# v's block means reach batch 0's last four token tiles by two DMAs, and the later weights are issued behind these

## The chip, the cores and the metric

The kernel runs on one core of a Trainium2 chip. A core has four compute engines that run their own instruction queues: TensorE (PE in the profile, with its weight loads as PEld), VectorE (DVE), ScalarE (ACT) and GpSimd (POOL). SyncE (SP) issues nearly all DMAs, in order: an issue whose condition isn't met holds up every issue behind it. The metric is the device time of one execution in microseconds, the median of several runs.

## The reference

Three blocks follow each other, for 2 batches of 768 tokens. First an attention with 8 heads of 64: each token sees the keys less than 16 away from it, and beside these 24 block summaries, one for each block of 32 keys (the maximum of the keys, the mean of the values). Then a feed-forward block with a token shift (512 to 1024 to 512) and a gate; then a mixer over tokens (768 to 256 to 768) and one over channels (512 to 1536 to 512).

```python
k_sum = k.reshape(B, H, nb, block, D).max(axis=3)
v_sum = v.reshape(B, H, nb, block, D).mean(axis=3)
scores_all = np.concatenate([scores_l_m, scores_s], axis=-1)   # local, then summaries
a = softmax(scores_all); out = a @ np.concatenate([v, v_sum], axis=2)
xk = mu_k * x + (1.0 - mu_k) * x_prev
k = np.maximum(xk @ w_k, 0.0); v = k * k @ w_v
r = sigmoid(xr @ w_r); x = r * v
u = x + (np.maximum(x.T @ w_tok1, 0.0) @ w_tok2).T
out = u + np.maximum(u @ w_ch1, 0.0) @ w_ch2
```

## The kernel before

**Tiles and stages.** A batch is 6 token tiles of 128. In the attention a unit of batch 0 is one token tile with every other head (`e` = 0 or 1), 12 units in all; a unit of batch 1 is a token tile with both. A unit passes through these steps: scores on TensorE (`sp`, L367), a masked read with row maxima on VectorE (L385), exponentials on ScalarE (L387), four transposes on TensorE (`pt`, L405) and their copy out of PSUM (`PT`, L408 on ScalarE for `e` = 0, L410 on VectorE for `e` = 1), and the products with the values (`pv`, L425). In batch 0 the sums of the softmax are divided out at the end (`rb`, L441, and the normalised tile `xT`, L445); in batch 1 GpSimd scales the probabilities (L399). Scores have two PSUM banks.

**Values and their means.** Each half of a token tile needs its own matrix of 120 rows: 96 rows of v (64 tokens and 16 more on either side) and 24 rows of block means. For batch 0 the 12 matrices lie in `ybuf`, two for a token tile. `vw_load` (L329) brings v's 96 rows. The means come from one sum of v over blocks (`vt_sum`, `v_gather`), which gives `vs`, 24 x 512, and `copy_sums` puts `vs` into each matrix, at row 0 or 96: token tile 0 by ScalarE, the others by GpSimd (first half, L345) and VectorE (second half, L343). In batch 1 each matrix gets its means by a DMA of its own.

**Weights.** They come as 64-bit floats. A piece of 128 x 512 is 512 KB; `Weights.load` (L137) issues its DMA on SP, and `Weights.step` turns it into a pair of 32-bit pieces, high and low: a prelude on ScalarE (L153), two integer operations on VectorE (L157, L163), the high half on ScalarE (L174) and the low half on GpSimd (L175). A product is three matmuls (high by high, high by low, low by high). The first 16 pieces are w_k (even numbers) and w_v (odd numbers) of the feed-forward block. `mixed` prepares that block's input (tmp on GpSimd L530, xk and xl on VectorE, xh on ScalarE); its products are ko (with w_k) and acc (with w_v); between them stand rl (VectorE), kh (ScalarE) and kl (GpSimd, L556).

**What sets the order.** The program is written stage by stage, with generators that interleave attention and feed-forward block; the framework then sorts the instructions of each engine by its own estimate of times and by the priorities that `ahead` gives. Engines run in the resulting order. The DMAs of SP use eight semaphores in turn, so each waits for the end of the one eight before it. In the order before, SP issues keys, queries and v for the first token tiles, then for each of the token tiles 2 to 5 two weights, two v halves and a q tile, then the other eight weights, then batch 1's keys, queries and values.

Of the kernel before, what the change touches and what calls it, by code (L numbers as in the profile page):

```python
# [30 lines left out]
AHEAD = 4  # L31
SPIN0 = 7
SPIN, SPIN_UNITS = 1, 8
WFIRST = 2
S2COST, S3COST, S4COST = 4, 2, 3
PT_ACT = ((0, 0), (1, 0), (1, 1))
GB = 4
# [12 lines left out]
AHEAD3 = 2  # L50
WF = 2
HC = 256
VSUM = 0, 2
OB = 2

# [2 lines left out]
def fused_kernel(ctx, tc, q, k, v, vt, mu, w_k, w_v, w_r, w_t1, w_t2, w_c1, w_c2, out):  # L58
    nc = tc.nc
    B, NT = q.shape[:2]  # L60
    S, DM = v.shape[1] - WINDOW * 2, v.shape[2]
# [5 lines left out]
    NB = S // BLOCK  # L67
# [13 lines left out]
    def bank(tag, bufs, shape, name):  # L81
        return ps.tile(shape, F32, tag=tag, bufs=bufs, name=name)
# [10 lines left out]
    ybuf = ypool.tile([128, B * NT, DM], F32, name="ybuf")  # L93
# [6 lines left out]
    class Slot:  # L100


        def __init__(self, pl, tag):
            self.pl, self.tag = pl, tag
# [16 lines left out]
    class Weights:  # L121


        def __init__(self):
            self.todo, self.loaded, self.rounded, self.pin, self.ahead = [], [], [], 0, AHEAD
            self.early = True

        def add(self, slot, src, use):
            self.todo.append((slot, src, use))
# [1 line left out]
        def load(self):  # L131
            if self.todo:
                slot, src, use = self.todo.pop(0)
                slot = slot.next()
                st = slot.tile([128, 512], I64, "wst")
                w = src.shape[2] if len(src.shape) > 2 else 0
                d = nc.sync.dma_start(st.rearrange("p (a n) -> p a n", n=w) if w else st, src)  # L137
                if PINW:
                    after(d)
                self.loaded.append((slot, st, use))  # L140

        def step(self):
# [35 lines left out]
    def pieces(slot, name):  # L178
        return [x.rearrange("p (a n) -> p a n", n=HC) for x in slot.split(name)]

    def sums(pair, eng, *ops, adder=nc.vector):
        s = stage.tile([128, 512], F32, tag="wf", bufs=WF, name="sum")
        s = s.rearrange("p (a n) -> p a n", n=HC)
        for a, x, y, op in ops:
# [42 lines left out]
    def behind(inst, marks):  # L227

        for m in marks:
            tc.add_manual_dep(inst.ins, m.ins.name,  # L230
                              mybir.DependencyInfo(mybir.DependencyClass.NoSync, mybir.DependencyReason.DATA), reason="queue order")

    def after(inst):

        behind(inst, mark[-1:])

    weights = Weights()
# [17 lines left out]
    def ahead(n):  # L255

        def wrap(fn):
            def run(*args, **kw):
                with tc.high_priority(n) if n else ExitStack():
                    return fn(*args, **kw)  # L260
            return run
        return wrap

    state = {}
# [24 lines left out]
    @ahead(HK)  # L289
    def kw_sums(b, t):  # L290
        st = state[b]
        for o in (0, WC - NB):
            nc.gpsimd.tensor_scalar(st["kw"][t][:, :, o:o + NB], st["ks"], 1.0, 1.0, ALU.mult, ALU.mult)
# [10 lines left out]
    @ahead(HR)  # L304
    def vt_sum(b, j):
        st = state[b]
        if j == 0:
            st["vr"] = at.tile([128, NP, NB], F32, tag="vrs", bufs=1, name="vrs")
        r = nc.vector.tensor_reduce(st["vr"][:, 2 * j:2 * j + 2], st.pop(("vt", j)), AX.X, ALU.add)
        if b == 0:  # L310
            behind(r, lows[-1:])

    @ahead(HR)
    def v_gather(b):
        st = state[b]
        vp = bank("pt", 2, [128, NP, 128], "vp")
        for p in range(NP):
            nc.tensor.transpose(vp[:NB, p], st["vr"][:, p], ident)
        st["vs"] = at.tile([NB, DM], F32, tag="vs", bufs=1, name="vs")
        nc.scalar.activation(st["vs"], vp[:NB].rearrange("p g e -> p (g e)"), AF.Copy, scale=1.0 / BLOCK)  # L320

    @ahead(HL)
    def vw_load(b, t):
        ws = []
        for half in range(2):
            w = ybuf[:NC, 2 * t + half] if b == 0 else at.tile([NC, DM], F32, tag="vw", bufs=VB, name="vw")
            row, srow = (NB, 0) if half == 0 else (0, NK)
            key = 128 * t + 64 * half
            after(nc.sync.dma_start(w[row:row + NK], v[b, key:key + NK]))  # L329
            ws.append((w, srow))  # L330
        st_of(b)["vw"][t] = ws

    def vw_sums(b, t):
        ahead(HV if b or t == 0 else 0)(copy_sums)(b, t)

    def copy_sums(b, t):
        for j, (w, srow) in enumerate(state[b]["vw"][t]):
            if b:
                nc.sync.dma_start(w[srow:srow + NB], state[b]["vs"])
            elif t == 0:  # L340
                nc.scalar.copy(w[srow:srow + NB], state[b]["vs"])
            elif j:
                nc.vector.tensor_copy(w[srow:srow + NB], state[b]["vs"])  # L343
            else:
                nc.gpsimd.tensor_copy(w[srow:srow + NB], state[b]["vs"])  # L345

    @ahead(HL)
    def q_load(b, t):
# [100 lines left out]
    def attention():  # L449
        slots = {}  # L450
        n0 = 2 * NT
        steps = [(0, t, (e,)) for t in range(NT) for e in range(2)] + [(b, t, (0, 1)) for b in range(1, B) for t in range(NT)]
        for i in range(len(steps) + 1):
            if i < len(steps):
                b, t, es = steps[i]
                if b and t == 0:
                    yield from prep(b)
                zs = s_stage(b, t, es)
                if len(es) == 1:
                    for what, z, lag in zip((t_stage, v_stage), (zs[0], zs), LAGS):  # L460
                        slots.setdefault(min(i + lag, n0), []).append(((i + lag, lag), what, z))
                else:
                    slots[i + 1] = [((i, 1), n_stage, z) for z in zs] + [((i, 2), t_stage, z) for z in zs] + [((i, 3), v_stage, zs)]
                if i < SPIN_UNITS:
                    spin(SPIN)
                yield 0.95 * len(es)
                if es[-1] == 1 and t + 1 < NT:
                    kw_sums(b, t + 1)
                if b and t == 0:
                    vw_sums(b, 0)  # L470
                if i in VSUM:
                    vt_sum(0, VSUM.index(i))
                if i == VSUM[1]:
                    v_gather(0)
                    vw_sums(0, 0)
            for _, what, z in sorted(slots.get(i, ()), key=lambda s: s[0]):
                what(z)
                if what is t_stage:
                    yield 0.43
                elif what is v_stage:  # L480
                    yield 0.7 * len(z)
                    done_tiles[0] += len(z) / 2
            if i < len(steps):
                if 0 in es:
                    if t + 1 < NT and t + 1 not in state[b]["vw"]:
                        vw_load(b, t + 1)
                    if b and t + 2 < NT:
                        q_load(b, t + 2)
                if i == VSUM[1]:
                    vw_sums(0, 1)  # L490
                elif 1 in es and t + 1 < NT and i > VSUM[1]:
                    vw_sums(b, t + 1)
                if b + 1 < B:
                    for e in es:
                        prep_next(b + 1, 2 * t + e)
# [16 lines left out]
    def prep(b):  # L512

        for t in range(NT):
            k_max(b, t)
            yield HOLD / (NT + 2)
        for j in range(2):
            vt_sum(b, j)
            yield HOLD / (NT + 2)
        kw_sums(b, 0)  # L520
        v_gather(b)
# [23 lines left out]
    def cut(p, a, n):  # L545
        return p[0][:, a:a + n], p[1][:, a:a + n]
# [69 lines left out]
    def spin(n):  # L616

        o = bank("ko", 1, [128, 4, 128], "spin")
        for _ in range(n):
            after(nc.tensor.matmul(o, ident, ident.unsqueeze(1).to_broadcast([128, 4, 128]), start=True, stop=True))  # L620
# [13 lines left out]
    for t in range(2, NT):  # L634
        for _ in range(WFIRST):
            weights.load()
        vw_load(0, t)
        if t + 1 < NT:
            q_load(0, t + 1)
    while weights.todo:  # L640
        weights.load()
    masks = []
    for kind in range(3):
        mc = at.tile([128, NC], F32, name=f"mask{kind}")
# [96 lines left out]
    def c1_src(g, z):  # L741
        return w_c1[z * 128:(z + 1) * 128, :].rearrange("p (h f) -> p h f", h=2)[:, :, HC * g:HC * g + HC]

# [88 lines left out]
    def new_f4():  # L832
        return w2.tile([128, 4, HC], F32, tag="f4", bufs=2, name="f4")

# [85 lines left out]
    def d_phase(uu):  # L920
# [9 lines left out]
        def part(i, g, uu):  # L930
            seq[0] += 1
            o = bank(*(("ko", 1), ("pv", 1), ("pt", 2), ("pt", 2))[seq[0] % 4], [128, 2, HC], "m")
            while (i, 1) not in c1[g]:
# [5 lines left out]
        def values2(pr, c, g, fh, th, last=False):  # L939
# [6 lines left out]
            for j, f in enumerate(fs):  # L946
                wh, wl = c2[c, f]
                for n in range(2):
                    t = 2 * th + n
                    gh, gl = cut(pr, j * HC + n * 128, 128)  # L950
                    for i, (l, r) in enumerate(((gh, wh), (gh, wl), (gl, wh))):
# [188 lines left out]
```

## Time and profile before

| | |
|---|---|
| median of 3 runs | 505.56 us (503.67 to 506.71) |
| the profiled execution | 506.84 us |
| its span, first to last instruction | 504.9 us |
| TensorE busy | 489.1 us, 97% |
| VectorE / ScalarE / GpSimd busy | 319.6 / 239.7 / 240.0 us |
| mean granted clock of TensorE | 0.989 |

A share of busy time is a mean over stages. TensorE is full almost everywhere, so what can move the end is its idle time and the time at a lower clock; both lie in the first 100 us, but for the last few. A waiting engine names what released it last, and a DMA issue is shown on SP with the time at which it left.

### The profile page before, as it was taken

Reading aid. Unit: us, or ns where it says so; the run is one execution under the profiler, and the core shown is the slowest. Engines: PE = TensorE matmul, PEld = TensorE weight load, DVE = VectorE, ACT = ScalarE, POOL = GpSimd, SP = SyncE. Lnnn points to the kernel's source line nnn. Section 1 sums busy time; section 2 is a strip of 40 time slices with the busy share of each in tenths; the row PEclk is TensorE's granted clock in tenths of the full one; section 3 lists DMA queues with packets and bytes.
Section 4 is the critical chain, followed back from the end, with each engine's and each line's share of the span. In section 5 each row is a group of like instructions: output and inputs, shape, how many; then the busy total and the mean of one; then the engine's idle time right before and its main releaser. Section 6 shows DMA issues by size and latency. Waiting matters only on the chain.

```text
span 504.9 us, 8793 instructions
## 1 busy us (share of the span) xinstructions
PE 489.1 (97%) x3278; PEld 407.0 (81%) x3278; DVE 319.6 (63%) x638; ACT 239.7 (47%) x541; POOL 240.0 (48%) x294
## 2 busy tenths in 40 slices
PE   7999997999999999999999999999999999999996
PEld 3567785888888898887887787878888999989995
DVE  3888998641514365698789789646479638354352
ACT  1778746872443545655456555554554435011110
POOL 5335587862543457488845535764941813000000
PEclk9899998899999999999999999999999999999999
DMA  8999940321000650000550999629351404163102
GB/s 265 298 294 345 345 124 13 89 80 40 20 1 1 233 186 0 1 0 7 162 167 5 386 398 329 215 91 320 132 167 42 140 30 167 51 201 112 56 1 83
DMA packets 35914, 70.63 MB, mean 140 GB/s; under 512 B 3072, under 2 KB 12288, under 8 KB 35872
## 3 DMA queue, kind: packets, MB, share of 16 engines
q1 hardware_dynamic: 34288, 69.09, 42.1%
q10 hardware_dynamic: 1584, 0.98, 0.7%
q8 instruction: 26, 0.43, 0.4%
q14 instruction: 16, 0.13, 0.1%
HBM read 60.04 MB, written 9.44 MB: 138 GB/s over the span
## 4 chain that ended last, share of the span: by engine, by line
PE 65%; DVE 14%; DMA 11%; ACT 4%; POOL 3%; issue 3%; SPq 1%; DVEq 0%; ACTq 0%; POOLq 0%
PE o L952 12%; PE ko L541 11%; PE m L541 11%; PE acc L541 10%; PE o L980 7%; PE go L541 5%; DMA wst<-in_moe_w_v_dram 4%; PE ro L541 3%; DVE wf L163 3%; DMA wst<-in_moe_w_ch_dram 2%; DMA xT<-in_vt_dram 2%; DVE xk L531 2%; PE pv L425 2%; PE sp L367 2%; DVE xl L533 2%
## 5 line engine op out<-in xcount | busy, mean ns | idle before, releaser
L175 POOL TENSOR_TENSOR w<-wf,w 128x512 fp32r<-128x512 f32 x50 | 69.0, 1387 | 60.8 <-ACT w L174 57.7
L541 PE MATMUL ko<-xh,w 128*128 128x256 f32 x384 | 76.4, 288 | 1.7 <-POOL w L175 0.9
L541 PE MATMUL m<-u,w 128*128 128x256 f32 x504 | 65.1, 283 | 0.7 <-DVE mw L843 0.7
L541 PEld LDWEIGHTS m<-u,w 128*128 128x128 f32 x504 | 63.4, 191 | 2.8 <-DVE mw L843 0.9
L541 PEld LDWEIGHTS ko<-xh,w 128*128 128x128 f32 x384 | 61.2, 188 | 5.4 <-POOL w L175 1.1
L541 PE MATMUL acc<-w,kh 128*128 128x512 f32 x192 | 61.4, 404 | 0.0
L952 PE MATMUL o<-w,gh 128*128 128x512 f32 x192 | 59.1, 391 | 0.0
L541 PE MATMUL ko<-xl,w 128*128 128x256 f32 x192 | 54.4, 283 | 1.1 <-DVE xl L533 1.1
L174 ACT CAST w<-wf 128x512 fp32r<-128x512 f32 x50 | 30.9, 620 | 50.3 <-DVE wf L163 48.5
L163 DVE SCALAR_TENSOR_TENSOR wf<-wst,wf 128x512 int32<-128x512 int32 x50 | 47.5, 958 | 8.8 <-ACT wst L153 7.7
L556 POOL TENSOR_TENSOR kl<-rl,kh 128x512 fp32r<-128x512 f32 x24 | 34.3, 1430 | 36.0 <-ACT kh L555 32.6
L530 POOL TENSOR_SCALAR tmp<-xT,oms 128x256 f32<-128x256 f32 x52 | 38.5, 748 | 21.2 <-DVE xk L531 12.4
L554 DVE TENSOR_TENSOR rl<-rl 128x512 f32<-128x512 f32 x24 | 18.7, 781 | 46.0 <-ACT rl L553 45.8
L387 ACT ACTIVATE pe<-pe,mn 128x120 f32<-128x120 f32 x96 | 36.6, 383 | 14.8 <-DVE mn L385 14.6
L531 DVE SCALAR_TENSOR_TENSOR xk<-xT,mus,tmp 128x256 f32<-128x256 f32 x52 | 39.3, 788 | 5.1 <-POOL tmp L530 4.7
L153 ACT ACTIVATE wst<-wst 128x512 f32<-128x512 f32 x62 | 40.9, 674 | 2.7 <-DMA wst<-in_moe_w_ch_dram 2.7
L541 PEld LDWEIGHTS acc<-w,kh 128*128 128x128 f32 x192 | 35.3, 192 | 7.3 <-ACT pe L387 0.3
L952 PEld LDWEIGHTS o<-w,gh 128*128 128x128 f32 x192 | 34.7, 188 | 6.2
L541 PE MATMUL acc<-w,kl 128*128 128x512 f32 x96 | 37.8, 404 | 0.9 <-POOL kl L556 0.9
L541 PEld LDWEIGHTS ko<-xl,w 128*128 128x128 f32 x192 | 36.2, 188 | 2.2 <-DVE xl L533 1.3
L952 PE MATMUL o<-w,gl 128*128 128x512 f32 x96 | 37.1, 391 | 0.0
L541 PE MATMUL go<-u,w 128*128 128x512 f32 x144 | 35.7, 393 | 0.0
(119 smaller groups left out, 950.9 us busy)
## 6 DMA issues: line engine op xcount, KB each, us to landing
wst<-in_moe_w_ch_dram SPq DMA_DIRECT2D x36, 512.0 KB, 7.3
w<-stored SPq DMA_DIRECT2D x24, 512.0 KB, 5.5
stored<-w SPq DMA_DIRECT2D x24, 256.0 KB, 4.8
wst<-in_moe_w_k_dram SPq DMA_DIRECT2D x8, 512.0 KB, 7.9
wst<-in_moe_w_v_dram SPq DMA_DIRECT2D x8, 512.0 KB, 9.9
wst<-in_moe_w_tok_dram SPq DMA_DIRECT2D x6, 512.0 KB, 4.9
out_dram<-o SPq DMA_DIRECT2D x12, 256.0 KB, 2.3
kw<-in_k_dram SPq DMA_DIRECT2D x9, 320.0 KB, 5.0
```

What stands on the lines that cost most here:

```text
L153: a = nc.scalar.activation(top.bitcast(F32), top.bitcast(F32), AF.Prelu, scale=2.0 ** -112, alpha=2.0 ** 32)
L163: nc.vector.scalar_tensor_tensor(wi, top, 3, wi, ALU.logical_shift_left, ALU.bitwise_or)
L174: r = nc.scalar.copy(hi, src)
L175: eng.tensor_tensor(lo, src, hi.bitcast(F32), ALU.subtract)
L387: nc.scalar.activation(pe, pe, AF.Exp, bias=mn[:, p:p + 1], scale=-1.0, accum_out=den[:, p:p + 1])
L530: nc.gpsimd.tensor_scalar(tmp, xT[:, d, x0 - 1:x0 - 1 + MW], om[:, d:d + 1], 1.0, ALU.mult, ALU.mult)
L531: nc.vector.scalar_tensor_tensor(xk[:, d], xT[:, d, x0:x0 + MW], mu[:, d:d + 1], tmp, ALU.mult, ALU.add)
L541: nc.tensor.matmul(o, l, r, start=(first and i == 0), stop=(last and i == 3 * n - 1))
L554: nc.vector.tensor_tensor(rl, rl, rl, ALU.mult)
L556: nc.gpsimd.tensor_tensor(lo, rl, hi.bitcast(F32), ALU.subtract)
L952: nc.tensor.matmul(accs[c][t], l, r, start=(first and j == 0 and i == 0), stop=(last and j == 1 and i == 2))
L980: nc.tensor.matmul(accs[0][t], l, r, start=(k == 0 and i == 0), stop=(k == NF2 - 1 and i == 2))
```

## The change

`copy_sums` still writes the means of token tile 0 by ScalarE and of tile 1 by GpSimd and VectorE. For token tiles 2 to 5 it issues, together with tile 0's copies, two DMAs on SP: one writes `vs` four times to row 0 of the four first halves, one to row 96 of the four second halves (192 KB each). The second for-loop of the start issues one weight instead of two ahead of each token tile's values; the remaining 12 are issued in the attention's third step, and each is put behind the second of the two DMAs in the queue (`gate`).

```diff
-WFIRST = 2
+WFIRST = 1
+TV = 2
...
                 if PINW:
                     after(d)
+                behind(d, self.gate)
...
     def copy_sums(b, t):
         for j, (w, srow) in enumerate(state[b]["vw"][t]):
+            vs = state[b]["vs"]
             if b:
-                nc.sync.dma_start(w[srow:srow + NB], state[b]["vs"])
+                nc.sync.dma_start(w[srow:srow + NB], vs)
             elif t == 0:
-                nc.scalar.copy(w[srow:srow + NB], state[b]["vs"])
+                nc.scalar.copy(w[srow:srow + NB], vs)
+                weights.gate = [nc.sync.dma_start(ybuf[srow:srow + NB, 2 * TV + j:2 * NT:2],
+                                                  vs.unsqueeze(1).to_broadcast([NB, NT - TV, DM]))]
...
                 if i == VSUM[1]:
                     v_gather(0)
                     vw_sums(0, 0)
+                    while weights.todo:
+                        weights.load()
...
                 if i == VSUM[1]:
-                    vw_sums(0, 1)
-                elif 1 in es and t + 1 < NT and i > VSUM[1]:
+                    for j in range(1, TV):
+                        vw_sums(0, j)
+                elif b and t + 1 < NT:
                     vw_sums(b, t + 1)
...
-    while weights.todo:
-        weights.load()
```

The order on SP is then: keys, queries, v of the first tiles; a weight, two v halves and a q tile three times; a weight and two v halves; batch 1's first key tile; the two DMAs of the means; 12 weights; batch 1's other loads. The sorting gives other orders on the engines too.

VectorE before, just behind the first weight's second operation (`wf_472`); `ybuf` is the matrices of values, `dens` a softmax sum, `pe_458` the masked scores of the sixth unit:

```order
L436 TENSOR_SCALAR dens_305<-dens_305 128x8
L163 SCALAR_TENSOR_TENSOR wf_472<-wst_119,wf_472 128x512
L343 COPY ybuf_71<-vs_326 24x512
L437 RECIPROCAL dens_305<-dens_305 128x8
L343 COPY ybuf_71<-vs_326 24x512 x4
L385 ISA pe_458,mn_457<-sp_448,mask0_162 128x120
```

VectorE in the change, the same place:

```order
L441 TENSOR_SCALAR dens_281<-dens_281 128x8
L165 SCALAR_TENSOR_TENSOR wf_472<-wst_119,wf_472 128x512
L348 COPY ybuf_71<-vs_302 24x512
L442 RECIPROCAL dens_281<-dens_281 128x8
L390 ISA pe_458,mn_457<-sp_448,mask0_138 128x120
```

Four copies are gone from ahead of the sixth unit's scores. VectorE before, between the scores of the seventh unit and those of the eighth (`pe_620`); `xT` is the first normalised token tile:

```order
L385 ISA pe_531,mn_520<-sp_511,mask0_162 128x120
L385 ISA mn_520 128x1
L445 TENSOR_TENSOR xT_84<-xT_84,rb_391 128x4x128
L385 ISA pe_620,mn_619<-sp_610,mask0_162 128x120
L385 ISA mn_619 128x1
```

VectorE in the change, the same place; `kw_445` is batch 1's first key tile, which the DMA ahead of the means brings:

```order
L390 ISA pe_529,mn_518<-sp_509,mask0_138 128x120
L390 ISA mn_518 128x1
L450 TENSOR_TENSOR xT_84<-xT_84,rb_393 128x4x128
L289 TENSOR_REDUCE ks_446<-kw_445 128x4x4
L390 ISA pe_618,mn_617<-sp_608,mask0_138 128x120
L390 ISA mn_617 128x1
```

The maximum over that key tile has moved up to here, from behind the first normalised input of the feed-forward block. GpSimd before, around the key sums of batch 1 (`kw<-ks`, twelve copies); `w_828` is weight 9's low half, `w_835` weight 10's, `w_935` weight 11's:

```order
L556 TENSOR_TENSOR kl_643<-rl_641,kh_642 128x512
L175 TENSOR_TENSOR w_828<-wf_824,w_828 128x512
L293 TENSOR_SCALAR kw_445<-ks_446 128x4x24 x2
L293 TENSOR_SCALAR kw_608<-ks_446 128x4x24 x2
L293 TENSOR_SCALAR kw_793<-ks_446 128x4x24 x2
L293 TENSOR_SCALAR kw_997<-ks_446 128x4x24 x2
L293 TENSOR_SCALAR kw_1105<-ks_446 128x4x24 x2
L293 TENSOR_SCALAR kw_1107<-ks_446 128x4x24 x2
L556 TENSOR_TENSOR kl_758<-rl_756,kh_757 128x512
L175 TENSOR_TENSOR w_835<-wf_831,w_835 128x512
L175 TENSOR_TENSOR w_935<-wf_931,w_935 128x512
```

GpSimd in the change, the same place; here `w_824` is weight 9's, `w_831` weight 10's, `w_929` weight 11's and `w_952` weight 12's:

```order
L564 TENSOR_TENSOR kl_641<-rl_639,kh_640 128x512
L177 TENSOR_TENSOR w_824<-wf_820,w_824 128x512
L177 TENSOR_TENSOR w_831<-wf_827,w_831 128x512
L295 TENSOR_SCALAR kw_445<-ks_446 128x4x24 x2
L295 TENSOR_SCALAR kw_606<-ks_446 128x4x24 x2
L295 TENSOR_SCALAR kw_789<-ks_446 128x4x24 x2
L295 TENSOR_SCALAR kw_991<-ks_446 128x4x24 x2
L295 TENSOR_SCALAR kw_1099<-ks_446 128x4x24 x2
L295 TENSOR_SCALAR kw_1101<-ks_446 128x4x24 x2
L564 TENSOR_TENSOR kl_754<-rl_752,kh_753 128x512
L177 TENSOR_TENSOR w_929<-wf_925,w_929 128x512
L177 TENSOR_TENSOR w_952<-wf_948,w_952 128x512
```

Weight 10 stands ahead of the key sums instead of behind them, and weight 12 follows 11 at once. Behind these rows the change has one kl, four scalings of probabilities (L404), two tmp, three scalings, weight 13, a scaling, a tmp and weight 14; before it were two tmp, weight 12, two tmp, weight 13, a kl, four scalings and weight 14.

## Rows read from the trace of the kernel before

Nothing is left out of a row; "..." stands for rows between.

**Rows 1.** Busy time by stretch: stretch, its length, each engine's busy us, clock, DMA

```profile
24.00:30.00 6.00, 6.00 (x56) 3.67 (x52) 5.89 (x15) 3.53 (x12) 4.49 (x5) 1.00 1.08 299
...
42.00:48.00 6.00, 6.00 (x91) 5.10 (x90) 6.00 (x26) 5.50 (x21) 4.62 (x5) 1.00 1.02 369
...
84.00:90.00 6.00, 4.99 (x38) 3.47 (x39) 5.82 (x30) 4.86 (x20) 3.39 (x5) 0.52 0.19 43
```

**Rows 2.** TensorE's waits, 24 to 100 us: waiter, releaser, total us, times, longest

```profile
PE sp L367 <- issue: 1.5, 1, 1.5
PE ko L541 <- DVE xl L533: 1.1, 1, 1.1
PE pt L405 <- DVE PT L410: 1.0, 1, 1.0
PE ko L541 <- POOL w L175: 0.9, 1, 0.9
PE ko L541 <- ACT rl L553: 0.8, 1, 0.8
```

**Rows 3.** Timeline of TensorE: start us, us, line, operation, idle before

```profile
42.97 1.04 PE L367 MATMUL sp<-kw,xT 64*64 64x120 f32 x18
...
66.38 1.09 PE L541 MATMUL acc<-w,kh 128*128 128x512 f32 x4
...
80.63 0.39 PE L541 MATMUL ko<-xh,w 128*128 128x256 f32 x1 [0.77 <-ACT rl L553]
...
82.04 0.50 PE L541 MATMUL ko<-xh,w 128*128 128x256 f32 x2 [0.91 <-POOL w L175]
...
85.57 2.07 PE L541 MATMUL acc<-w,kh 128*128 128x512 f32 x4
...
92.12 0.28 PE L541 MATMUL ko<-xh,w 128*128 128x256 f32 x1
...
93.39 1.04 PE L367 MATMUL sp<-kw,qT 64*64 64x120 f32 x30
```

**Rows 4.** Chain of waits, 137 to 143 us: start us, us, what

```profile
137.22 3.04 PE ko L541 x24
140.26 2.80 PE acc L541 x12
```

**Rows 5.** Timeline of GpSimd

```profile
23.31 3.94 POOL L345 COPY ybuf<-vs 24x512 f32<-24x512 f32 x5 [2.55 <-ACT vs L320]
...
73.57 1.26 POOL L556 TENSOR_TENSOR kl<-rl,kh 128x512 fp32r<-128x512 f32 x1
...
74.80 2.98 POOL L175 TENSOR_TENSOR w<-wf,w 128x512 fp32r<-128x512 f32 x2
...
79.63 0.96 POOL L530 TENSOR_SCALAR tmp<-xT,oms 128x256 f32<-128x256 f32 x2 [1.86 <-DVE xT L445]
...
80.56 1.43 POOL L175 TENSOR_TENSOR w<-wf,w 128x512 fp32r<-128x512 f32 x1
...
89.44 1.39 POOL L399 TENSOR_SCALAR pe<-pe,den 128x120 f32<-128x120 f32 x4 [2.61 <-DVE den L396]
...
90.79 2.52 POOL L175 TENSOR_TENSOR w<-wf,w 128x512 fp32r<-128x512 f32 x2
```

**Rows 6.** Timeline of VectorE

```profile
21.66 0.43 DVE L157 TENSOR_SCALAR wf<-wst 128x512 int32<-128x512 int32 x1 [0.39 <-DMA wst<-in_moe_w_k_dram]
...
25.53 3.57 DVE L343 COPY ybuf<-vs 24x512 f32<-24x512 f32 x4
...
33.94 0.68 DVE L445 TENSOR_TENSOR xT<-xT,rb 128x512 f32<-128x512 f32 x1
...
42.71 1.02 DVE L157 TENSOR_SCALAR wf<-wst 128x512 int32<-128x512 int32 x1
```

**Rows 7.** Timeline of SP's DMA issues

```profile
24.07 0.55 SPq L353 DMA_DIRECT2D xT<-in_q_dram  x1
...
45.61 5.75 SPq L280 DMA_DIRECT2D kw<-in_k_dram  x3
```

More of the change, by code (lines that the diff above doesn't have):

```diff
@@ L125, in __init__ @@
             self.todo, self.loaded, self.rounded, self.pin, self.ahead = [], [], [], 0, AHEAD
-            self.early = True
+            self.early, self.gate = True, []
         def add(self, slot, src, use):
@@ L337, in copy_sums @@
         for j, (w, srow) in enumerate(state[b]["vw"][t]):
+            vs = state[b]["vs"]
             if b:
-                nc.sync.dma_start(w[srow:srow + NB], state[b]["vs"])
+                nc.sync.dma_start(w[srow:srow + NB], vs)
             elif t == 0:
-                nc.scalar.copy(w[srow:srow + NB], state[b]["vs"])
+                nc.scalar.copy(w[srow:srow + NB], vs)
+                weights.gate = [nc.sync.dma_start(ybuf[srow:srow + NB, 2 * TV + j:2 * NT:2],
+                                                  vs.unsqueeze(1).to_broadcast([NB, NT - TV, DM]))]
             elif j:
-                nc.vector.tensor_copy(w[srow:srow + NB], state[b]["vs"])
+                nc.vector.tensor_copy(w[srow:srow + NB], vs)
             else:
-                nc.gpsimd.tensor_copy(w[srow:srow + NB], state[b]["vs"])
+                nc.gpsimd.tensor_copy(w[srow:srow + NB], vs)
     @ahead(HL)
```

## The prediction, made before the changed kernel ran

> **What bounds the kernel now.** I read the table of busy time by stretch first. From 24 to 48 us, four stretches of 6 us, TensorE is busy for all of each at the full granted clock (the first and the last are shown); in 84 to 90 it is at 0.52 [rows 1]. Then the list of TensorE's waits between 24 and 100 us: five, 5.3 us together (1.5 + 1.1 + 1.0 + 0.9 + 0.8) [rows 2]. Outside these TensorE is the bound, so only work that ends one of them earlier moves the end.
>
> TensorE's timeline places them. Two (on xl and on PT) lie between 48 and 54 us, where the feed-forward block's first products begin. The other three lie in one hole, 80 to 85 us, around the fourth group of ko products, which wants weights 12 and 14 (I number the w_k and w_v pieces 0 to 15 in the order of their loads). The product that waits for weight 12 starts at 82.04; the four acc products at 85.57 take 2.07 us where four such took 1.09 at 66.38, so this is the lower of the two clock levels, 1.2 GHz; the product that needs weight 14 starts at 92.12 [rows 3].
>
> How much does the hole cost? Between 80.63 and 92.12 TensorE does twelve ko products, twelve acc products and a unit of scores. At the full clock the chain of waits shows 24 ko in 3.04 us and 12 acc in 2.80 [rows 4], and 30 records of scores take 1.04 [rows 3]: 1.5 + 2.8 + 1.0 = 5.3 us. The hole costs 11.5 - 5.3 = 6.2 us.
>
> GpSimd's timeline says who is late: weight 12's low half ends at 80.56 + 1.43 = 81.99 and weight 14's at 90.79 + half of 2.52 = 92.05, each within 0.1 us of the product [rows 3, 5]. So the hole is GpSimd's queue: the twelve copies of key sums, one kl (1.26), weights 10 and 11 (2.98), and only then weight 12.
>
> **The change, part by part.** *Removed:* four of VectorE's five copies and four of GpSimd's five. The four on VectorE are one row of 3.57 us at 25.53 [rows 6]; GpSimd's five are 3.94 us, so four are 3.15 [rows 5]. GpSimd's are hidden: it is busy for 4.49 of the 6 us there [rows 1]. VectorE's hold back the score reads behind them, but TensorE, which has no gap there, has older work to do: in the program its transposes of one unit stand where VectorE reads the scores of a unit three later. So 0 directly, and at most the 2.1 us of the two waits at 48 to 54.
>
> *Added:* two transfers of 192 KB, and a new order. Weight 0 has landed at 21.66, when VectorE stops waiting for it [rows 6]. Each DMA on SP is released by the end of the one eight before it; so the issue at 24.07 answers to weight 1's end, the one at 45.61 to weight 8's, and 5,888 KB lie between: 273 KB/us [rows 7]. At that rate a weight takes 1.87 us, a v half-tile 0.70, a q tile 0.94, a k tile 1.17. In the new order (v, v, q, weight three times, v, v, k of batch 1, the block means, then weights) weight 1 lands at 25.8, 2 at 30.0, 3 at 34.2, k at 36.8, the block means at 38.2, weight 4 at 40.1, 5 at 41.9; in the old order 4 and 5 come out at 34.4 and 36.2 by the same rate. For the block means no row exists. The nearest is v's half-tile of equal bytes, 0.70 each, which I take; the bounds are 0 (bytes that never leave the chip) and 1.87 each, a whole weight's.
>
> By the Trainium skill (DMA: Bandwidth & Descriptors, section "Why a DMA increments its semaphore by 16 and not by 1"), a transfer runs on the largest number of engines up to 16 that divides its slowest dimension, so on 12 for 24 partitions. Each would then last as long as 256 KB on 16, by estimate 0.94 us, and every later weight would land 0.5 us later. No run here shows it.
>
> *Waits it adds.* In the new order VectorE takes the maximum over batch 1's first key tile right behind the first normalised token tile, which ended at 33.94 + 0.68 = 34.6 [rows 6]. The keys land at 36.8, so VectorE stands for 2.2 us, and a unit of score reads, weight 3 and the next normalised tile are queued behind it. Weight 4 then stands ahead of that tile: reached about 38.9, landed 40.1, 1.2 us more. On ScalarE the preludes of weights 2 and 3 stand ahead of a unit's exponentials, which come 1 to 2 us late. TensorE feels none of this until it wants a bank of scores that VectorE hasn't read: that is the unit whose products start at 42.97 [rows 3], and VectorE is through with the bank at 41 to 43. I take 0; the bounds are 0 and +1.5. SP's gate costs nothing: GpSimd could read the means from 23.31 on [rows 5], and SP comes to their DMA only when weight 2 has landed, at 30.0.
>
> *48 to 54.* VectorE has 3.57 us of copies less and 3.4 of stalls more and comes out level. The transpose that waited 1.0 for a copy out of PSUM stands about 1 us later still, while one unit of transposes moves behind the first ko products. I take +0.5; the bounds are -2.1 (both waits gone) and +2.5.
>
> *54 to 92.* One maximum is already done, and GpSimd's order now has weight 10 ahead of the key sums. With these ending at 73.57 as before, kl and weights 11 and 12 behind them end at 73.57 + 1.26 + 2.98 = 77.8 instead of 81.99, before TensorE gets there at 80. Weight 14 is then behind another kl (1.27), eight scalings of probabilities (1.39 / 4 = 0.35 each, 2.8), three tmp (0.96 / 2 = 0.48 each, 1.4) and weight 13: 77.8 + 1.3 + 2.8 + 1.4 + two weights of 1.43 = 86.2 [rows 5]. With 1.5 for waits on VectorE's reciprocals between them it is 87.7, against 92.05. Gain 4.3. The bounds are 6.2, the whole hole, and 0, if what GpSimd needs from VectorE comes 4 us later.
>
> *After 92.* Only orders within a stage differ, and 384 KB more (1.4 us) lie in transfers that hide behind the products. 0.
>
> Sum: 0 + 0.5 - 4.3 = -3.8. Against the profiled execution, 506.84 (504.9 of span, 1.9 around it), that is 503.0. The median of the runs shown, 505.56, stands 1.28 below that execution, so I predict 501.8.
>
> **Rivals.** *The stalls eat it (no change).* If v, v, q go slower than the mean rate and weights faster, weight 4 lands past 42 and VectorE's two stalls add up to 5 instead of 3.4 us. The feed-forward block begins 2 us late, VectorE hands its maxima to GpSimd 2 us late, and of the 4.3 some 2 remain, less 1 before 54: 504.6. For it: VectorE is busy for all of 42 to 48 [rows 1], so it can't catch up. Against it: the 3.57 us it saves come ahead of the stalls.
>
> *A second hole (slower).* ScalarE takes the preludes of weights 4 and 5 in its queue ahead of two units' exponentials. If weight 5 lands later than about 44, these come 3 us late, TensorE runs out of transposes, and a hole like that of 80 to 85 opens at 42 to 54: 3 us of idle time, then the lower clock, at which products double (2.07 for 1.09 [rows 3]), 2 us over a stretch. Price 5, less 2 kept at the later hole: 508.6. For it: weight 4 lands 5.7 us later than in the old order. Against it: it was read only at 42.71 there [rows 6], 8 us after it landed.
>
> *The means come too late.* TensorE wants token tile 2's means near 41. At 1.87 us each the two transfers land at 40.5, so only a rate below the bound would hold it up, at 1 us per us: 503 to 504. The change then isn't the saving that it says.
>
> **How the numbers follow.** Forecast 0.48 (498.5 to 503.5), stalls 0.27 (503 to 506), second hole 0.15 (507 to 511), late means 0.10 (502 to 506). About 0.5%, 2.5 us, is what a measurement of this kernel can tell from no change, so faster means below 503.0 and slower above 508.1. Faster: 0.42 of the forecast, 0.05 of the stalls, 0.04 of the late means, 0.51. Slower: 0.12 of the second hole, and 0.05 for later orders that I haven't followed, 0.17. Same: 0.32. The range, 498.3 to 508.0, leaves out the worse half of the second hole and gains beyond 7 us.
>
> **What would show it.** Right: VectorE's maximum of batch 1's first key tile waits for a DMA at 34 to 37; TensorE has no wait from 24 to 48; the product with weight 12 has none near 80; the one with weight 14 starts at 86 to 89; no stretch is at half clock. Wrong: a TensorE wait over 1.5 us before 54, the hole at 80 to 85 still there, or weight 14 past 90.

## The result: 1.2% slower, and where the time went

| | before | change |
|---|---|---|
| median (4 runs each, taken together) | 504.94 us | 511.37 us (510.05 to 512.58) |
| ratio | | 1.0122 [1.0097, 1.0147] |
| profiled execution / its span | 506.84 / 504.9 | 511.6 / 509.8 |
| TensorE busy / mean granted clock | 489.1 / 0.989 | 494.2 / 0.985 |
| VectorE, GpSimd busy | 319.6, 240.0 | 319.0, 233.8 |

The forecast was 501.8 (498.3 to 508.0). GpSimd was busy for 6.2 us less, of which its four copies are 3.15 [rows 5], and the end came 4.9 us later in the span. Before's executions took 503.5 to 504.4 us where the mean granted clock was 1.000 and 506.2 to 509.3 at 0.989, so its profiled one, at 0.989, is among its longer, and the spans are 4.9 us apart where the medians are 6.4. The line that grew is TensorE's own busy time, by 5.1 us, with the same 3278 products:

```profile
PE 494.2 (97%) x3278; PEld 410.3 (80%) x3278; DVE 319.0 (63%) x634; ACT 239.3 (47%) x541; POOL 233.8 (46%) x290
```

TensorE's waits between 24 and 100 us answer to [rows 2]: 5.5 us instead of 5.3, but at other places.

```profile
PE acc L549 <- POOL kl L564: 1.8, 1, 1.8
PE sp L372 <- DVE mn L390: 1.7, 1, 1.7
PE pv L430 <- DVE PT L415: 1.3, 1, 1.3
PE pv L430 <- ACT PT L413: 0.7, 1, 0.7
```

The table by stretch of the change, against [rows 1]. The last three columns are the granted clock, the DMA share and GB/s.

```profile
24.00:30.00 6.00, 6.00 (x63) 4.02 (x63) 1.51 (x12) 3.85 (x13) 1.27 (x1) 1.00 1.09 276
30.00:36.00 6.00, 6.00 (x58) 4.00 (x57) 3.63 (x13) 3.23 (x8) 1.51 (x2) 1.00 1.09 252
36.00:42.00 6.00, 4.28 (x49) 3.19 (x49) 3.35 (x13) 4.21 (x18) 1.03 (x1) 0.88 1.05 311
42.00:48.00 6.00, 6.00 (x58) 4.94 (x56) 5.65 (x25) 4.37 (x14) 4.66 (x6) 0.55 1.03 408
...
54.00:60.00 6.00, 5.88 (x51) 5.55 (x52) 5.86 (x12) 5.75 (x16) 2.79 (x2) 0.72 1.09 368
...
78.00:84.00 6.00, 4.24 (x22) 2.91 (x21) 6.00 (x21) 2.95 (x10) 6.00 (x8) 0.79 0.00 0
84.00:90.00 6.00, 6.00 (x52) 4.96 (x51) 4.71 (x11) 4.44 (x16) 3.71 (x9) 0.92 0.16 37
```

VectorE is busy for 1.5 and 3.6 of 6 us between 24 and 36, where it was 5.9 [rows 1] and, by the same view, 4.6 before, and the stretch 42 to 48, where TensorE did 91 products at the full clock [rows 1], now has 58 at 0.55. A clock of 0.55 over 6 us, between levels of 1 and one half, means 5.4 us at the half level; the five stretches below 1 add up to 1.4 + 5.4 + 3.4 + 2.5 + 1.0 = 13.7 us. Before had 10.2: 5.8 in the stretch at 0.52 [rows 1], and by the same view 3.4 at 12 to 18 us (0.72) and 1.1 at 90 to 96 (0.91). The difference, 3.5 us at half speed, costs 1.7.

Three places tell the story. The first is VectorE's stall, with TensorE's wait behind it (VectorE's rows first, from its timeline, then TensorE's):

```profile
33.23 0.68 DVE L450 TENSOR_TENSOR xT<-xT,rb 128x512 f32<-128x512 f32 x1
38.55 0.69 DVE L289 TENSOR_REDUCE ks<-kw 128x16 f32<-128x512 f32 x1 [4.64 <-DMA kw<-in_k_dram]
39.15 0.27 DVE L390 CUSTOM_DVE_ANT_0 pe<-sp,mask 128x120 f32<-128x120 f32 x1
...
41.10 0.43 DVE L159 TENSOR_SCALAR wf<-wst 128x512 int32<-128x512 int32 x1
41.45 0.68 DVE L450 TENSOR_TENSOR xT<-xT,rb 128x512 f32<-128x512 f32 x1
```

```profile
37.84 0.63 PE L372 MATMUL sp<-kw,xT 64*64 64x120 f32 x8
40.19 0.39 PE L372 MATMUL sp<-kw,xT 64*64 64x120 f32 x2 [1.72 <-DVE mn L390]
...
42.93 1.97 PE L430 MATMUL pv<-PT,ybuf 120*64 120x64 f32 x16
```

VectorE waits 4.64 us for batch 1's first keys. The scores queued behind that maximum keep both banks, so TensorE, which wanted a bank at 38.47, stands until 40.19. Then come the windows at 0.88 and 0.55. The row at 41.10 is VectorE's first operation on weight 4, without a wait.

The second place is the hole of 80 us, still there. The chain of waits from 72 us on (start, us, what):

```profile
72.36 0.89 DVE wf L159
73.25 0.60 DVE ks L289
73.86 0.08 issue
73.94 2.42 POOL kw L295 x3
...
77.53 1.20 POOL kw L295 x5
78.73 1.24 POOL kl L564
79.97 0.04 issue
80.02 2.56 PE acc L549 x8
```

VectorE's last key maximum (`ks`) ends at 73.85, the key sums stand behind it, kl behind those, and TensorE waits 1.8 us for kl. In [rows 5] the same kl began at 73.57, 5.2 us earlier.

The third place has no wait in it. TensorE's timeline at 91 us:

```profile
91.28 0.42 PE L372 MATMUL sp<-kw,qT 64*64 64x120 f32 x2
91.63 0.32 PE L410 MATMUL pt<-ident,pe 128*120 128x128 f32 x1
91.88 0.42 PE L372 MATMUL sp<-kw,qT 64*64 64x120 f32 x2
92.23 0.33 PE L410 MATMUL pt<-ident,pe 128*120 128x128 f32 x1
92.48 0.43 PE L372 MATMUL sp<-kw,qT 64*64 64x120 f32 x6
```

Two scores and a transpose take 0.60 us from start to start, twice. Thirty scores in one piece took 1.04 [rows 3], so two are 0.07; a transpose is at most the 0.33 of its row. At least 0.2 us of each 0.60, which holds two switches, is neither. I call it a switch when TensorE's order goes from products with 64-column weight tiles (sp, pv, rb) to the others (pt, ko, acc) or back: before has 94 of them, the change 110. By the Trainium skill (TensorEngine Tiling (Array Packing), section "Key Properties"), changing the tiling mode drains the engine, changing the tile alone does not. These rows agree; the page gives no figure, the experiments do. My count is by columns alone, and TensorE's timeline of the kernel before shows that it leaves some out:

```profile
40.38 0.65 PE L405 MATMUL pt<-ident,pe 128*120 128x128 f32 x4
40.96 0.42 PE L367 MATMUL sp<-kw,xT 64*64 64x120 f32 x2
41.31 1.15 PE L425 MATMUL pv<-PT,ybuf 120*64 120x64 f32 x16
```

From two scores (64 rows by 64 columns) to the products with the values (120 by 64) it takes 0.35 us from start to start, just as from two scores to a transpose above. Counted with these the kernel before has 105 switches, the change 120, and before_fewer_switches and change_fewer_switches (below) 65 and 66.

### The profile page after: what moved, and what is told of

Same layout as the page of the kernel before. It is cut to its first block, busy times and chain, and to the rows that moved or that the text cites. A ratio compares the mean times of both kernels' runs of the same rounds, so it can differ in the third digit from the quotient of the medians.

```text
span 509.8 us, 8784 instructions
## 1 busy us (share of the span) xinstructions
PE 494.2 (97%) x3278; PEld 410.3 (80%) x3278; DVE 319.0 (63%) x634; ACT 239.3 (47%) x541; POOL 233.8 (46%) x290
## 4 chain that ended last, share of the span: by engine, by line
PE 71%; DVE 11%; DMA 9%; ACT 3%; POOL 2%; issue 2%; SPq 1%; DVEq 0%; ACTq 0%
PE o L958 12%; PE acc L549 11%; PE ko L549 11%; PE m L549 11%; PE o L986 6%; PE go L549 5%; DMA xT<-in_q_dram 5%; PE ro L549 5%; PE sp L372 3%; PE pv L430 2%; DVE wf L165 2%; DMA kw<-in_k_dram 2%; PE pt L410 2%; DVE xk L539 2%; PE h L549 2%
## 5 line engine op out<-in xcount | busy, mean ns | idle before, releaser
L549 PEld LDWEIGHTS ko<-xh,w 128*128 128x128 f32 x384 | 61.4, 188 | 2.5 <-issue 0.8
L549 PE MATMUL acc<-w,kh 128*128 128x512 f32 x192 | 60.1, 398 | 0.0
L538 POOL TENSOR_SCALAR tmp<-xT,oms 128x256 f32<-128x256 f32 x52 | 36.0, 702 | 22.9 <-DVE xk L539 13.8
L562 DVE TENSOR_TENSOR rl<-rl 128x512 f32<-128x512 f32 x24 | 20.4, 851 | 38.1 <-ACT rl L561 37.9
L392 ACT ACTIVATE pe<-pe,mn 128x120 f32<-128x120 f32 x96 | 36.6, 384 | 15.6 <-DVE mn L390 15.6
```

What stands on the lines that cost most here:

```text
L392: nc.scalar.activation(pe, pe, AF.Exp, bias=mn[:, p:p + 1], scale=-1.0, accum_out=den[:, p:p + 1])
L538: nc.gpsimd.tensor_scalar(tmp, xT[:, d, x0 - 1:x0 - 1 + MW], om[:, d:d + 1], 1.0, ALU.mult, ALU.mult)
L549: nc.tensor.matmul(o, l, r, start=(first and i == 0), stop=(last and i == 3 * n - 1))
L562: nc.vector.tensor_tensor(rl, rl, rl, ALU.mult)
```

## The experiments

Ratios are to the kernel before, run on the same chip beside each. Some kernels keep every instruction's place on the four engines by a table (called pinned below), so that only what is named differs; the rows of such a kernel all have one line number, and one reads them by tile. The theories: VectorE's stall at 34 to 39 us costs the time (A in the expectations); the switches cost it (S); the late key maxima cost it (K).

| kernel | median us (runs) | ratio [95%] | switches |
|---|---|---|---|
| the change | 511.37 (4) | 1.0122 [1.0097, 1.0147] | 110 |
| max_later | 508.99 (7) | 1.0074 [1.0046, 1.0102] | 100 |
| key_last | 509.48 (7) | 1.0097 [1.0062, 1.0132] | 106 |
| engine_copies | 511.27 (5) | 1.0109 [1.0078, 1.0141] | 114 |
| wfirst2_key_last | 506.99 (12) | 1.0043 [1.0015, 1.0072] | 96 |
| change_old_orders | 506.32 (12) | 1.0022 [1.0006, 1.0038] | 94 |
| dma_means_old_orders | 509.93 (6) | 1.0094 [1.0068, 1.0120] | 94 |
| before_fewer_switches | 500.16 (6) | 0.9916 [0.9886, 0.9946] | 58 |
| change_fewer_switches | 503.65 (12) | 0.9970 [0.9954, 0.9986] | 60 |
| change_unstalled | 508.88 (7) | 1.0068 [1.0043, 1.0094] | 110 |
| change_old_fewer | 502.89 (11) | 0.9949 [0.9929, 0.9968] | 58 |
| change_both_cures | 503.29 (12) | 0.9963 [0.9946, 0.9981] | 60 |
| before_fewer_pool | 500.71 (6) | 0.9907 [0.9873, 0.9942] | 58 |
| change_94 | 509.14 (7) | 1.0074 [1.0046, 1.0102] | 94 |
| change_94_unstalled | 508.55 (11) | 1.0057 [1.0030, 1.0084] | 94 |
| change_three | 509.35 (12) | 1.0071 [1.0041, 1.0102] | 94 |

**First round: four edits that leave the sorting free.** The maximum behind the first `xl`:

```diff
-        nc.vector.tensor_reduce(st["ks"][...], keys, AX.X, ALU.max)
+        d = nc.vector.tensor_reduce(st["ks"][...], keys, AX.X, ALU.max)
+        if b:
+            behind(d, lows_x[:1])      # lows_x: the list of xl operations
```

> The DMA order stays as in the change; only VectorE's maximum over batch 1's first key tile is put behind the first normalised input of the feed-forward block (xl), where it stood before. Theory A (that maximum makes VectorE stand 4.64 us, from 33.9 to 38.55, and the two later half-clock stretches follow from it): the TensorE wait of 1.7 us at 40.19 and the half clock of 40 to 47 are gone, 504 to 507 us. Theory B (weights 2 and 3 land too late for ScalarE, which waits 2.30 and 2.57 us for them): 510 to 512 as with the change. Theory C (the block means' transfers themselves): 510 to 512.

Measured 508.99, between the ranges of all three theories. VectorE now waits as long for the next thing in its queue, weight 4 (VectorE's and TensorE's timelines):

```profile
40.74 0.43 DVE L159 TENSOR_SCALAR wf<-wst 128x512 int32<-128x512 int32 x1 [4.70 <-DMA wst<-in_moe_w_k_dram]
```

```profile
42.59 0.62 PE L413 MATMUL pt<-ident,pe 128*120 128x128 f32 x4 [1.49 <-DVE xT L453]
```

The stall moved rather than went, and the order has 10 switches fewer besides: it tells the theories apart poorly.

Batch 1's first keys behind all weights:

```diff
+        d = q.dma_start(kw[:, :, K0:K0 + 2 * HALF], k[b, t])
+        if b:
+            behind(d, weights.last)
```

> As the change, but batch 1's first key tile is loaded behind all weights, so the means and the weights land about 1.2 us earlier and the maximum falls back to its place behind xl. Theory A (the maximum's wait on VectorE is what costs): like the kernel with the maximum later, 503 to 507 us. Theory B (weights 2 and 3 too late on ScalarE): these two land as before, 509 to 512. Theory C (the means' transfers): 510 to 512.

Measured 509.48, in the range of theory B alone. Weight 4 is read at 38.80 after 3.04 us of waiting, TensorE has no wait over 0.40 us from 40 to 48, and one of 1.77 us at 50.23, again behind `xT`.

The copies back on the engines, with the change's order of DMAs:

```diff
-                nc.scalar.copy(w[srow:srow + NB], vs)
-                weights.gate = [nc.sync.dma_start(ybuf[...], vs.unsqueeze(1).to_broadcast(...))]
+                weights.gate = [nc.scalar.copy(w[srow:srow + NB], vs)]
...     # and vw_sums for token tiles 2 to 5 where they stood before
```

> No DMA of the means: all copies by VectorE and GpSimd as before, but one weight per token tile at the start and 12 weights behind batch 1's first key tile, as in the change. Theory A: VectorE is 3.1 us later at the maximum and the keys land at about 38, so its stall is 1.5 to 2 us shorter but what stands behind it comes as late: 508 to 512 us. Theory B: 509 to 512. Theory C (the transfers of the means are what costs): 504 to 506.

Measured 511.27, the change's time, but not by its waits: 0.52 us at 40, 2.12 at 51.55, and 3.69 at 85.60 for GpSimd, which has its copies back, with 114 switches in TensorE's order. Inconclusive: an edit re-sorts all the engines, and equal times here are two different kernels.

Two weights per token tile again, and the keys last:

```diff
-WFIRST = 1
+WFIRST = 2
+            behind(d, weights.last)      # as in key_last
```

> The means come by the two DMAs, but two weights go ahead of each token tile's values as before, and batch 1's keys come behind all weights. VectorE and GpSimd lose their four copies each. Theory A and theory B both: no stall on VectorE, no late weight, 502 to 505 us; theory B has it clearly (3 us or more) below the kernel with the key tile last and one weight per tile, theory A has the two within 2 us. Theory C: 508 to 512.

Measured 506.99, 2 us above the range of theories A and B, with 96 switches and, in the profiled execution, of 510.96 us, a wait of 2.99 us at 54.30. Over these five sorted orders the time falls with the switches (114 and 110 at 511.3, 106 at 509.5, 100 at 509.0, 96 at 507.0), which gave the second theory; five points that differ in much else don't show it.

**Second round: the orders pinned.** The change's DMAs with all four engines in before's order, less the eight copies:

```diff
+    TEN, VEC, SCA, GPS = (Kept(nc.tensor, PE_T, "PE"), Kept(nc.vector, DVE_T, "DVE"), ...)
+    # each instruction queued behind the one that the table puts ahead of it
```

> The change's DMAs in the change's order on SP (one weight per token tile, batch 1's first key tile, the means, 12 weights), but TensorE, VectorE, ScalarE and GpSimd each run in the order of the kernel before, less the eight copies. Theory O (the new orders cost, not the later landings): 503 to 507 us, no stall of VectorE over 2 us between 33 and 41. Theory L (weights 2 to 5 land 4 to 6 us later, and that costs in any order): 509 to 513.

Measured 506.32, 1.0022: the DMAs, their landings and the copies removed together cost 0.2%, by the interval at most 0.4. All else of the 1.2% lies in the new orders. The time is theory O's, but VectorE does stand there, and for ScalarE (VectorE's timeline):

```profile
38.81 0.17 DVE L144 TENSOR_SCALAR dens<-dens 128x8 f32<-128x8 f32 x1 [3.83 <-ACT pe L144]
```

TensorE's longest wait between 36 and 48 us is 0.75 all the same: a stall of VectorE costs by what stands behind it. The windows of this kernel (columns as above) are at the full clock where the change's were not:

```profile
36.00:42.00 6.00, 5.38 (x81) 4.41 (x80) 2.86 (x5) 4.92 (x20) 1.68 (x2) 1.00 1.04 295
42.00:48.00 6.00, 5.04 (x73) 4.14 (x74) 6.00 (x30) 5.29 (x18) 5.21 (x6) 1.00 1.03 409
```

Two weights per token tile as before and batch 1's keys behind all weights, old orders:

```diff
-WFIRST = 1
+WFIRST = 2      # on change_old_orders
...
+            behind(d, weights.last)      # as in key_last
```

> Means by the two DMAs, two weights per token tile as before and batch 1's keys behind all weights; all four engines in the order of the kernel before, less the eight copies. It shows what the copies alone are worth. Theory O and theory L: 502 to 506, at most 2 us below before (the two waits at 48 to 54). If the means' transfers themselves cost, 507 or more.

Measured 509.93, above the 502 to 506 of theories O and L. The means leave SP at 34.97 instead of 30.71 in change_old_orders and land too late (TensorE's timeline):

```profile
42.25 0.30 PE L144 MATMUL pv<-PT,ybuf 120*64 120x64 f32 x2 [2.14 <-ACT pe L144]
43.57 1.76 PE L144 MATMUL pv<-PT,ybuf 120*64 120x64 f32 x14 [1.02 <-DMA ybuf<-vs]
```

The view puts the first of these waits down to ScalarE; that the means end it too is inferred, from the same two products waiting for them in change_both_cures below. With the keys out of the way the means still leave 4.3 us later, so it is one weight fewer per tile that makes their DMAs bearable.

Now TensorE's order alone, on before; what stands near its start (groups 21 to 39 of like products):

```diff
-sp x3, spin, sp, pv, sp x3, pv x15, pt x4, sp, spin, sp x8
-pv x8, pt, pv, pt, pv, pt, pv, pt, pv x5
+sp x8, spin, pv x16, pt x4, spin, sp x8
+pv x8, pt, pv x8, pt x3
```

> The kernel before with VectorE, ScalarE and GpSimd in their order and only TensorE's order changed: the products of one unit's scores or values are put together, so TensorE goes 58 times instead of 94 between products with 64-row or 64-column pieces (sp, pv, rb) and the others. Theory S (each such switch costs TensorE some 0.19 us, as an acc product between two pairs of pv takes 0.43 us against 0.23 between its like): up to 36 x 0.19 = 6.8 us less, of which some lies beside waits: 499 to 503. Without S: 504 to 507.

Measured 500.16, 0.9916. The same products, 36 switches fewer; the page's line of busy time, against 489.1 before:

```profile
PE 480.6 (96%) x3278; PEld 404.1 (81%) x3278; DVE 320.4 (64%) x638; ACT 239.2 (48%) x541; POOL 241.6 (49%) x294
```

By the time it is (505.8 - 500.16) / 36 = 0.16 us for one, with before's 505.8 on that chip. By the profiles it is somewhat more: of the 8.5 us less of busy time the clock (0.992 against 0.989 on the mean) accounts for some 1.6, which leaves 0.19 for one, and TensorE's idle time, span less busy, grew from 15.8 to 17.4. The same done to the change:

```diff
-# TensorE's order of the change: 110 switches
+# the same products, those of one form put together: 60
```

> The changed kernel with VectorE, ScalarE and GpSimd in their order and TensorE's products of a unit put together: 60 switches instead of 110. Theory S: up to 50 x 0.19 = 9.5 us less, 502 to 507. Without S: 510 to 513. The wait of 1.7 us for VectorE at 40 us should stay in both.

Measured 503.65, 7.7 us below the change for 50 switches, 0.155 each. Switches are a cost of their own: 16 of them are 2.5 us, two fifths of the 6.2 (1.22%) that the change lost.

**Third round: the stall, and both together.** Two moves on VectorE in the change's pinned order, TensorE's as it is:

```diff
 xT_84<-xT_84,rb_393
-ks_446<-kw_445
...
-wf_646<-wst_308
 xT_84<-xT_84,rb_498
...
+wf_646<-wst_308
 wf_646<-wst_308,wf_646
...
 xl_543
+ks_446<-kw_445
```

> The changed kernel with every engine in the change's order but for two moves on VectorE: the maximum over batch 1's first key tile goes behind the first xl, and the first operation on weight 4 goes from ahead of the second normalised tile to just ahead of its own second operation. DMAs as in the change. Theory O1 (what stands ahead of the score reads waits for a landing, and TensorE's wait at 40 and its 6.8 us at half clock follow): 505 to 508 us, full clock from 40 to 47. If only TensorE's switches make the change slow: 510 to 512.

Measured 508.88, 0.54% below the change and between the two ranges. The clock now holds to 42 us, and the hole opens later; its windows:

```profile
36.00:42.00 6.00, 6.00 (x86) 4.72 (x85) 3.02 (x13) 4.90 (x20) 2.03 (x4) 1.00 1.04 321
42.00:48.00 6.00, 5.07 (x72) 4.37 (x72) 6.00 (x18) 6.00 (x22) 3.98 (x4) 0.93 1.03 408
48.00:54.00 6.00, 4.70 (x39) 4.15 (x39) 6.00 (x23) 6.00 (x21) 2.56 (x2) 0.50 1.03 396
```

The change's DMAs, the old orders, and TensorE's with few switches; then the change's orders with few switches and no stall:

```diff
-PE_T of change_old_orders
+PE_T of before_fewer_switches      # change_old_fewer
...
-DVE_T of change_fewer_switches
+DVE_T of change_unstalled          # change_both_cures
```

> The change's DMAs, the engines in the order of the kernel before less the copies, and TensorE in the order with 58 switches. If orders are all and landings nothing, it is as much below the change in old orders (506.3) as the kernel before gained by the same TensorE order (5.6): 499.5 to 502. If the later landings leave less slack: 503 to 506.

> The changed kernel with 60 switches instead of 110 and with the two moves on VectorE. If stall and switches are two costs that add up: 503.7 less 3 to 5, 498.5 to 501. If the stall only costs where TensorE's order meets it: 502 to 504.

Measured 502.89 and 503.29. The first lies at the edge between its two expectations: its landings seem to leave less slack as TensorE gets faster: ScalarE stands 2.78 us at 34.91 for weight 3, and TensorE 2.22 at 39.13. In the second the cures don't add up, and here the means themselves are late (TensorE's timeline):

```profile
40.61 0.30 PE L143 MATMUL pv<-PT,ybuf 120*64 120x64 f32 x2 [1.23 <-DMA ybuf<-vs]
...
41.75 1.03 PE L143 MATMUL pv<-PT,ybuf 120*64 120x64 f32 x14 [0.84 <-DMA ybuf<-vs]
```

On before with few switches, GpSimd's weight 10 ahead of the last key sums and weight 12 right behind 11:

```diff
 kw<-ks x8
+w of weight 10
 kw<-ks x4
 kl
-w of weight 10
 w of weight 11
+w of weight 12
```

> The kernel before with 58 switches, and on GpSimd weight 10's low half behind eight of the twelve key sums instead of behind all and kl, weight 12's right behind weight 11's. The prediction's view that the hole at 80 to 92 is GpSimd's queue: weight 12 is done 2 us earlier, the half-clock stretch goes, 496 to 499. If another wait is right behind it: 499.5 to 501.

Measured 500.71: no gain over 500.16. Weight 12's wait went, and waits of 1.5 for kl and 1.9 for a maximum stand in its place.

**Last round: what is left of the new orders.** The scores of two units of batch 1 put together on TensorE, so that the change has before's 94 switches; the same without VectorE's stall; and that with the key maxima together on VectorE and the key sums ahead of weight 10 on GpSimd:

```diff
-sp x1 ... sp x3 ... sp, pt, sp, pt, sp x3, pt x2, sp x4, pt x2 ...  # TensorE
+sp x16 ... pt x6, ko x2, pt x2, pv x16 ...                          # change_94
...
-ks_446<-kw_445                            # VectorE: the two moves of change_unstalled
+...                                       # change_94_unstalled
...
+ks<-kw x5 (VectorE), kw<-ks x12 ahead of weight 10 (GpSimd)         # change_three
```

> The changed kernel, every order the change's, but the scores of two units of batch 1 put together on TensorE, so that it has the 94 switches of the kernel before instead of 110. Theory S (the 16 switches more are a cost of their own, 7.7 us / 50 = 0.155 us each by the runs so far): 2.5 us less than the change, 508 to 509.5. If the gain of fewer switches came from elsewhere: 510.5 to 512.

> The same with the two moves on VectorE as well. If stall (2.5) and extra switches (2.5) are the two costs and add up: 506 to 507, as the change's DMAs in the old orders (506.3). If they overlap, as with 60 switches: 508 to 509.

> The change with 94 switches and VectorE's two moves, and as a third: the last three maxima over batch 1's keys follow the third at once on VectorE, and GpSimd's twelve key sums stand ahead of weight 10 instead of behind it. Theory K (what is left over the old orders is the wait of 2.0 us for kl at 79, which stands behind key sums that start 4 us late): that wait goes or is under 0.5 us, 506 to 507. If another wait stands right behind it: 508 to 509.

Measured 509.14, as expected (2.2 us for 16 switches, 0.14 each); 508.55, where the sum of both cures would be 506.7; and 509.35, above both ranges. In change_94_unstalled TensorE waits 2.0 us for kl; in change_three that is gone (0.2) and the time isn't, since other waits took its place (TensorE's waits, 70 to 100 us):

```profile
PE pt L145 <- POOL pe L145: 1.6, 3, 1.2
PE ko L145 <- ACT rl L145: 1.6, 1, 1.6
PE ko L145 <- POOL w L145: 1.6, 1, 1.6
```

Theory K fell: taking away the wait behind the late key maxima gains nothing.

**The account.** Of the 1.22%, 0.22 are the DMAs with old orders, 1.00 the new orders. Within these VectorE's stall is worth 0.54 when cured alone, 16 switches 0.48 alone, both together 0.65. So some 0.35% (1.8 us) of the new orders has no cause that an experiment took away; the intervals of change_94_unstalled and change_old_orders overlap by a little, and it stays open. Their profiles say where to look: TensorE's idle time is 507.4 - 488.1 = 19.3 us in the first and 504.4 - 488.6 = 15.8 in the second, at a granted clock of 0.997 and 0.991, so it is waits, in many places, and not the clock. The profiles of before and the change give by themselves: idle time -0.2 (15.6 against 15.8), time at the lower clock +1.7, 16 switches at 0.155 +2.5, together 4.0 of the 4.9 us between the spans.

## Why the prediction was wrong

**"TensorE feels none of this until ... the unit whose products start at 42.97 ... I take 0; the bounds are 0 and +1.5."** This is the first step that failed. TensorE wanted the bank at 38.47. In before, too, there are scores ahead of 42.97, which the prediction passed over:

```profile
39.14 1.31 PE L367 MATMUL sp<-kw,xT 64*64 64x120 f32 x28
```

And the stall itself was 4.64 us where 2.2 was estimated: the keys landed at 38.5 instead of 36.8. The DMAs moved 276 and 252 GB/s between 24 and 36 us, not the mean of 273 KB/us, which is 280 in these units; that makes some 0.7 of the 1.7 us, and the rest has no row. The weights later went at 408. The condition of the rival "the stalls eat it" half came true: stalls near 5 us, but in one piece, and weight 4 was there by 41.10, not past 42. Its price did not: a wait of 1.7 us brought 6.8 us at the lower clock with it. The rival "a second hole" had the sign and half the size (508.6, 3 us above the median of 505.56), with the wrong engine: VectorE's queue opened it, not ScalarE's preludes. Curing the stall alone gave back 2.5 us.

**"With these ending at 73.57 as before."** The gain of 4.3 at the hole of 80 us rested on it. GpSimd's queue order was read rightly: weight 10 was done at 73 and weight 12 at 83.3. But the key sums wait for VectorE's last maximum, which ended at 73.85 where before had the last pair done at 68.65. The chain of the change runs through VectorE alone from 61.4 to 73.9, with 0.3 us of issue between: it had become the bound there. The prediction had named the risk in its lower bound ("if what GpSimd needs from VectorE comes 4 us later") and then taken the other end. The product that waited for weight 12 waits no more, and another one waits for kl at 80.02; weight 14's low half ends at 94.4, past the 90 that the prediction called a sign of being wrong. The hole was also laid too much to GpSimd. Of its 3.2 us of waits 0.9 name GpSimd [rows 2], and the product at 92.12 has no wait ahead of it [rows 3]: so weight 14's end at 92.05 held nothing up there. In before_fewer_pool the 0.9 went and nothing was gained.

**"After 92. Only orders within a stage differ ... 0."** An order within a stage is just what costs a switch. Of the 16 more 15 lie behind 92 us, and the 16 are 2.2 to 2.5 us by three pairs of kernels.

**"48 to 54 ... I take +0.5".** The bounds held: one wait of 1.28 for PT at 54.12 for the two of 2.1, then 3.4 us at the lower clock, which cost 1.7; together +0.9.

**Right:** that the copies removed and the DMAs, at the change's place, come to next to nothing (0.2% for both together in change_old_orders, which doesn't part them). "The means come too late" is real as soon as the means leave later (dma_means_old_orders) or TensorE is quicker (change_both_cures). In change_both_cures the two products that wait for them start 1.14 us apart, in dma_means_old_orders 1.32. That is nearer the 0.94 that the prediction worked out from the Trainium skill (DMA: Bandwidth & Descriptors, section "Why a DMA increments its semaphore by 16 and not by 1") than the 0.70 it took from v's half-tile; other transfers ran beside them, so no run shows the price of one alone.

## What to carry to other kernels

When an edit lets a scheduler sort again, the sorting is the change: pin the old orders first, to see what the edit alone is worth (here 0.2 of 1.2%). On a full TensorE count the switches between products of different tile form, since they cost time that no wait shows; before with 58 instead of 94 runs in 500.16 us and beats both kernels. And a queue that is put behind a landing is to be followed to every engine that needs what stands behind it, at the rate that the DMAs have in that stretch, not at a mean.

## What the runs showed that I had not expected

A switch between 64-column and 128-column tiles costs TensorE 0.16 us over 36 in before, 0.155 over 50 and 0.14 over 16 in the change, and appears as busy time. One between 64 and 120 rows at 64 columns (sp to pv) takes as long in the rows above.

The granted clock did not follow idle time alone. In the change TensorE was busy for 4.28 of the 6 us from 36 on, and the next six were at 0.55. Before was busy for 4.12 of 6 between 48 and 54, and its clock stayed at 1.00 there and in the next stretch; change_old_orders was at 5.38 and 5.04 and stayed at 1.00 too. What distinguishes them isn't settled by these runs.

Cures don't add up: 2.5 us for the stall and 2.2 for the switches were 2.8 together, as each cured wait had another right behind it.
